# Third pair's routing re-spread over the last attention steps, with its stores on SyncE and its scaling on GpSimd

## The chip, the cores and the metric

The kernel runs on one core of one Trainium2 chip. A core has five engines that run at the same time, each working through its own queue of instructions in order: TensorE (matrix products), VectorE, ScalarE, GpSimd and SyncE, which here only issues transfers. Times are device microseconds (us) of the whole program, launch to end; lower is better.

## The reference

Sliding-window causal attention (window 64) is followed by a mixture of experts without dropped tokens: each token goes to the one expert with its largest logit, through that expert's two-layer network, and the result is scaled by the softmax weight of that expert.

```python
# q, k, v: batch 8, heads 8, sequence 576, head size 64
scores = scale * np.matmul(q, k.transpose(0, 1, 3, 2))
scores = np.where((rel >= 0) & (rel < 64), scores, -1e9)
attn = softmax(scores);  attn_out = np.matmul(attn, v)
x = attn_out.transpose(0, 2, 1, 3).reshape(4608, 512)
logits = x @ w_gate                        # 8 experts
expert_idx = np.argmax(logits, axis=1)
gate_w = probs[np.arange(N), expert_idx]
for e in range(8):                         # rows sorted by expert
    h = np.maximum(x_sorted[lo:hi] @ w1[e], 0.0)     # 512 -> 1024
    y_sorted[lo:hi] = h @ w2[e]                      # 1024 -> 512
return gate_w[:, None] * y_sorted[inv_perm]
```

## The kernel before

**Attention.** The batch is worked on in four pairs (bg 0 to 3), the heads in four groups of two (g). A pair and a group are a unit, 16 in all, and a unit has three steps of three tiles of 128 queries (a pair has nine tiles): N = 48 steps, s = 0 to 47. The function step (line 1013) writes out by hand, under a manual schedule, what every engine gets in step s, as a software pipeline. In order:

- scored(s+1), the score products into PSUM banks 0 and 1 (TensorE, L700); masked(s+1), mask and row maximum (VectorE, L713); softened(s+1), the exponential (ScalarE, L723);
- weighted(s-1), the product with v (TensorE, L746); logit(s-3), the gate's logits (TensorE, L783);
- flipped(s): TensorE transposes the probabilities of both heads (L731), and the results are copied out of PSUM, head 0 by VectorE, head 1 by ScalarE (pT, L733);
- divided(s-1), division by the sum (VectorE, L756 to L760), into xs;
- loads of later units, all issued by SyncE (L615, L627, L631, L638), with copies of v by GpSimd (L639 to L645);
- turned(s+3), transposes of q and k (TensorE, L659 and L667, with copies on ScalarE, L662 and L672; the third step of a unit has only two transposes); x_turned(s-2), transposes of xs (TensorE L771, copy on ScalarE L774);
- what the list todo holds for this step.

Transposed blocks go to PSUM banks 2 to 5 in rotation (tr_ring): the fifth user waits until the first one's bank has been copied out.

**Routing.** When a pair's logits are complete, after() (L950) puts its routing into the todo lists of the following steps. choose(bg) is a generator of five parts: the maximum; the one-hot of the expert (oh_all) and the exponentials; rank products on TensorE (L833) and the gate weights (L843 to L845); ranks within experts (L850 to L860, the fourth part); and position (L862 to L870, the fifth part: rkhi, low). place(j) then builds two one-hot matrices of a tile (lo, L874), weigh scales a tile of xs by its gate weight (L883 on ScalarE, L885 on GpSimd) and store writes chunks of three tiles to x_dram (L894, L901). For the third pair (bg = 2) after() is called for step 39: parts at steps 39, 39, 40, 41 and 41, places at 42 to 44, scaling at 41 to 44 with two tiles (m = 2 and 6) on ScalarE, stores at 42 to 44 issued by GpSimd.

**The first table.** first_tiles (L974), at the end of step 45, finds the tokens of expert 0's first two tiles among the first three pairs: VectorE forms key and hi_e (L976, L979), TensorE multiplies lo with hi_e in 54 small products (L986), VectorE turns the slots into token numbers (perm_e, L989), and gather_first (L290) clears a buffer and fetches the tokens' rows from x_dram with an indirect DMA on GpSimd. The tokens numbered past the third pair are left out by a bounds check.

**After the loop.** turn() (L312) transposes the fetched rows (L316) and the first expert tile starts, interleaved with the rest of the attention and the last pair's routing. sums_w2(0) (L142, GpSimd) forms sums of expert 0's second weights, which SyncE loads in two halves at steps 42 and 45 (L1048, shown as L1036 in the trace since todo runs them). Then gather_first is called for the second tile. The experts' products are arranged as seven block products instead of eight (hidden and output, L354 and L398), and fill the time from about 210 us to the end.

Of the kernel before, what the change touches and what calls it, by code (L numbers as in the profile page):

```python
# [24 lines left out]
def _ins(ap: bass.AP, axis: int, n: int) -> bass.AP:  # L25

    dims = [list(d) for d in ap.ap]
    dims.insert(axis, [0, n])
    return bass.AP(tensor=ap.tensor, offset=ap.offset, ap=dims)


def _inner(ap: bass.AP, n: int) -> bass.AP:
    return _ins(ap, len(ap.ap), n)
# [3 lines left out]
def kernel(  # L37
# [10 lines left out]
    nc = tc.nc  # L48
    P = nc.NUM_PARTITIONS
    B, H, S, D = q.shape  # L50
# [9 lines left out]
    SM = NV * P  # L60
    BG = 2
    NTB = BG * S // P
# [40 lines left out]
    V, G = nc.vector, nc.gpsimd  # L103
# [51 lines left out]
    def sums_w2(e):  # L155
        form(right_sums(G, s2s[e % NW], *w2q(e)))
# [23 lines left out]
    with tc.tile_pool(name="tmp", bufs=1) as tmp:  # L180
# [8 lines left out]
        for i in range(BG):  # L189
# [12 lines left out]
            out=before[:], in_=ones[:], pattern=[[1, P]], compare_op=ALU.is_gt, fill=0.0, base=0,  # L202
# [42 lines left out]
    ST = 3  # L245
# [12 lines left out]
    xg_all = qk_m(0, C, DM)  # L258
    xg = [xg_all[:, c] for c in range(C)]
# [29 lines left out]

    def gather_first(tokens):  # L290

        for c in range(C):
            G.memset(xg[c], 0.0)

            G.indirect_dma_start(
                out=xg[c], out_offset=None, in_=x_dram[0 : NT - BG * S, :],
                in_offset=bass.IndirectOffsetOnAxis(ap=tokens[:, c : c + 1], axis=0),
                bounds_check=NT - BG * S - 1, oob_is_err=False,
            )
# [144 lines left out]
    NQ = P // QD  # L444

    def half_tile(e, blocks, after, next_x):

        w1, w2 = w1s[e % NW], w2s[e % NW]
# [119 lines left out]
    with tc.manual_schedule(), ExitStack() as held, ExitStack() as brief:  # L568
# [51 lines left out]
        def load_rests(bg):  # L620

            at = 6144 + bg % 2 * 2048
            vr = qk_m(at + 1024, BG, H, D)
            rests[bg] = [qk_m(at, H, D), qk_m(at + 512, H, D), vr]
            for t, src, queue in zip(rests[bg], (q, k), (nc.sync, nc.sync if bg else nc.scalar)):
                for i in range(BG):
                    queue.dma_start(  # L627
                        out=t[i * D : (i + 1) * D], in_=src[bg * BG + i, :, SM:S, :].rearrange("h p d -> p h d")
                    )
            for i in range(BG):  # L630
                nc.sync.dma_start(out=vr[D:P, i], in_=v[bg * BG + i, :, SM:S, :].rearrange("h p d -> p h d"))  # L631

        def load_v(u):
            bg, g = units[u]
# [39 lines left out]
        def blocks_of(t):  # L674

            return [(t // NV, t % NV * 2 + a) if t < BG * NV else (a, NB - 1) for a in range(2)]
# [42 lines left out]
        def softened(prs, mx):  # L719
            for h in range(2):  # L720
                for m in range(ST):
                    y = prs[h][:, m, :]
                    nc.scalar.activation(out=y, in_=y, func=AF.Exp, scale=-1.0, bias=mx[:, h, m : m + 1])  # L723
            return prs

        def flipped(prs):
            pTs = []
            for h in range(2):
                tr = banks[next(tr_ring)](0, ST, P)
                for m in range(ST):  # L730
                    nc.tensor.transpose(out=tr[:, m, :], in_=prs[h][:, m, :], identity=ident[:])  # L731
                pT = att.tile([P, ST, P], F32, name=f"pT{h}")
                (nc.scalar.copy if h else nc.vector.tensor_copy)(out=pT[:], in_=tr[:])  # L733
                pTs.append(pT)
            return pTs

        def weighted(s, pTs):
            u, c = divmod(s, NST)
            bg, g = units[u]
            va, vb = v_ring[u % NVR]  # L740
            px = banks[6 if s < N - 2 else s - N + 2](0, 2, ST, VW)
            for m in range(ST):
                for a, (bp, i) in enumerate(blocks_of(c * ST + m)):
                    vt = va[:, bp, i // 2] if i % 2 or i == 0 else vb[:, bp, i // 2 - 1]
                    for h in range(2):
                        nc.tensor.matmul(  # L746
                            px[a * D : (a + 1) * D, h, m, :], lhsT=pTs[h][:, m, a * D : (a + 1) * D],
                            rhs=vt[:, h, :], start=True, stop=True, skip_group_check=True,
                        )
            return px  # L750
# [25 lines left out]
        def logit(s):  # L776

            u, c = divmod(s, NST)
            bg, g = units[u]
            if g == 0 and c == 0:  # L780
                lgs[bg] = banks[7](0, NST, P)[0 : ST * GE]
            for m in range(ST):
                nc.tensor.matmul(  # L783
                    lgs[bg][m * GE : (m + 1) * GE, c, :], lhsT=wg[:, g, :], rhs=xTs[s][:, m * P : (m + 1) * P],
                    start=(g == 0 and c == 0), stop=(g == NG - 1), skip_group_check=True,
                )
            return g == NG - 1
# [113 lines left out]
                    engine.dma_start(out=x_dram[t0 + SM : t0 + S, :], in_=x[i * D : (i + 1) * D, ST - 1, :])  # L901

        gates = {}
        todo = {}


        def slot_table(hi):
# [42 lines left out]
        def after(s, routing, bg):  # L950

            do = lambda n, op: todo.setdefault(s + n, []).append(op)
            part = lambda: next(routing, None)
            if bg < last - 1:
                for n in range(5):
                    do(n, part)

                for m in range(NTB):
                    do(5 + m * 2 // 3, partial(place, bg * NTB + m))
                    do(5 + m * 2 // 3, partial(weigh, bg, m, G))  # L960
                    if m % ST == ST - 1:
                        do(5 + m * 2 // 3, partial(store, bg, m // ST, G))
                return

            for n in (0, 0, 1, 2, 2):
                do(n, part)
            for m in range(NTB):
                do(3 + m // 3, partial(place, bg * NTB + m))
                do((2, 2, 3, 3, 4, 4, 4, 5, 5)[m], partial(weigh, bg, m, nc.scalar if m in (2, 6) else G))
                if m % ST == ST - 1:  # L970
                    do(3 + m // ST, partial(store, bg, m // ST, G))
            do(6, first_tiles)

        def first_tiles():  # L974

            V.scalar_tensor_tensor(  # L976
                out=key[:], in0=rkhi[:, 0:NJE], scalar=1.0, in1=oh_all[:, 0, 0:NJE], op0=ALU.add, op1=ALU.mult
            )
            V.tensor_tensor(  # L979
                out=hi_e[:], in0=_inner(key[:], NE * C), in1=_ins(hi_id[:, C + 1 : C + 1 + NE * C], 1, NJE),  # L980
                op=ALU.is_equal,
            )
            slots = banks[next(tr_ring)](0, NE * C)
            for j in range(NJE):
                for i in range(2):
                    nc.tensor.matmul(  # L986
                        slots, lhsT=lo[:, i, j], rhs=hi_e[:, j], start=(i + j == 0), stop=(i + j == NJE)
                    )
            V.tensor_scalar(out=perm_e[:], in0=slots, scalar1=-1.0, scalar2=float(NT), op0=ALU.mult, op1=ALU.add)  # L989
            gather_first(perm_e[:, 0:C])  # L990

        N = NU * NST
        load_qk(0)
# [18 lines left out]
        prs, pTs = {}, {}  # L1012
        def step(s):
            if 0 <= s + 1 < N:
                prs[s + 1] = softened(*masked(s + 1, scored(s + 1)))
            if 0 <= s - 1 < N:
                px = weighted(s - 1, pTs.pop(s - 1))
            ripe = 0 <= s - 3 < N and logit(s - 3)
            if 0 <= s < N:
                pTs[s] = flipped(prs.pop(s))  # L1020
            if 0 <= s - 1 < N:
                divided(s - 1, px)
            if s >= 0 and s % NST == 0:
                u = s // NST
                if u + 3 < NU and (u + 3) % NG == 0:
                    load_rests((u + 3) // NG)
                if u + 2 < NU:
                    load_v(u + 2)
                if u + 3 < NU:
                    load_qk(u + 3)  # L1030
            if s + 3 < N:
                turned(s + 3)
            if 0 <= s - 2 < N:
                x_turned(s - 2)
            for op in todo.pop(s, ()):
                op()  # L1036
            if ripe:
                bg, c = (s - 3) // (NG * NST), (s - 3) % NST
                parts = by_tokens(bg, c)
                next(parts)  # L1040
                todo.setdefault(s + 1, []).append(partial(next, parts, None))
                if c == NST - 1:
                    after(s + 1, choose(bg), bg)
# [4 lines left out]
            todo.setdefault(s, []).append(partial(nc.sync.dma_start, out=w2s[0][:, fs], in_=w2v[0][:, fs]))  # L1048
        for s in range(-3, N):
            step(s)  # L1050
        assert not todo
        sums_w2(0)


# [45 lines left out]
        table = slot_table(hi)  # L1100
# [144 lines left out]
```

## Time and profile before

| | |
|---|---|
| runs of the kernel | 700.83, 703.4, 706.3 us; median 703.4 |
| the profiled execution | 701.35 us |
| its span, first to last instruction | 699.6 us |
| mean granted TensorE clock | 0.993 |
| TensorE busy with products | 674.8 us, 96% |
| VectorE, ScalarE, GpSimd busy | 504.4, 262.3, 356.3 us |
| TensorE busy, 123 to 165 us | 41.26 of 42 |
| TensorE busy, 172 to 190 us | 16.33 of 18 |
| TensorE busy, 190 to 205 us | 11.70 of 15, at clock 0.79 |
| TensorE busy, 236 to 700 us | 454.70 of 464 |

In the profile PE is TensorE's products, PEld its weight loads, DVE VectorE, ACT ScalarE, POOL GpSimd and SP SyncE. L986 is line 986 of the kernel. A name with q (SPq, POOLq) is the engine's instruction queue. In a timeline row stand the start, the duration, engine, line, operation, what is written and read, and in brackets the idle time before it and what ended that. In a row of waits stand the waiting engine and line, what it waited for, and the total, the number and the longest in us. In a row of windows stand the stretch, its length, the busy time of PE, PEld, DVE, ACT and POOL, the granted TensorE clock as a share of full speed, the busy share of the DMA engines, and GB/s.

### The profile page before, as it was taken

How to read it: one execution, taken by the hardware profiler on the slowest of the kernel's cores; microseconds unless marked ns; L12 is line 12 of the kernel's file. 1: busy time of each engine (PE TensorE's matmuls, PEld its weight loads, DVE VectorE, ACT ScalarE, POOL GpSimd, SP SyncE). 2: the span in 40 equal slices, each digit the busy share in tenths (PEclk: the TensorE clock that was granted, in tenths of full speed). 3: DMA queues.
4: the chain of work that ended last, by engine and by line, in shares of the span. 5: the costliest groups of instructions: out<-in, count | busy, mean ns of one | idle time of the engine just before them, and what ended most of it. 6: DMA issues, size and time to landing. Idle time of an engine off the chain costs nothing. (4 is left out here: it accounts for less than half of the span.)

```text
span 699.6 us, 18016 instructions
## 1 busy us (share of the span) xinstructions
PE 674.8 (96%) x6894; PEld 590.8 (84%) x6894; DVE 504.4 (72%) x1657; ACT 262.3 (37%) x665; POOL 356.3 (51%) x368
## 2 busy tenths in 40 slices
PE   5999999999989999999999999999999999999996
PEld 4888888878769898897999899899789799789995
DVE  3667898898966958774866776676767576776864
ACT  5888889878745211111211111121121121132211
POOL 5414659387475025946662167267255757254012
PEclk9999999999989999999999999999999999999999
DMA  9988789887342281451711163171226171111022
GB/s 201 220 207 190 180 194 237 209 203 197 126 163 81 92 297 61 142 210 37 259 60 63 31 226 106 33 269 63 64 88 240 50 254 64 64 38 58 6 62 61
DMA packets 137151, 94.52 MB, mean 135 GB/s; under 512 B 116591, under 2 KB 116607, under 8 KB 137024
## 3 DMA queue, kind: packets, MB, share of 16 engines
q1 hardware_dynamic: 114752, 36.19, 21.1%
q0 software_dynamic: 9120, 28.60, 12.7%
q10 hardware_dynamic: 13152, 28.05, 11.6%
q8 instruction: 78, 1.28, 0.7%
q14 instruction: 49, 0.40, 0.2%
HBM read 73.94 MB, written 20.45 MB: 135 GB/s over the span
## 5 line engine op out<-in xcount | busy, mean ns | idle before, releaser
L325 DVE STREAM_TRANSPOSE v_m<-qk_m 32x256 f32<-32x256 f32 x320 | 139.2, 435 | 6.9 <-DMA qk_m<-x_dram,at_g 0.9
L285 POOL DMA_INDIRECT qk_m<-x_dram,at_g x42 | 45.0, 1072 | 161.5 <-DVE v_m L325 152.6
L354 PE MATMUL bank<-qk_m,s 128*128 128x128 f32 x1024 | 122.4, 275 | 0.0
L354 PEld LDWEIGHTS bank<-qk_m,s 128*128 128x128 f32 x1024 | 118.3, 192 | 0.0
L723 ACT ACTIVATE pr<-pr,mx 128x128 f32<-128x128 f32 x288 | 89.6, 390 | 31.6 <-DVE mx L713 31.2
L354 PE MATMUL bank<-qk_m,w 128*128 128x128 f32 x768 | 94.1, 276 | 0.8 <-PEq L1150 0.5
L354 PEld LDWEIGHTS bank<-qk_m,w 128*128 128x128 f32 x768 | 90.3, 192 | 4.3 <-issue 4.0
L713 DVE CUSTOM_DVE_ANT_0 pr<-bank,mask 128x128 f32<-128x128 f32 x288 | 64.4, 286 | 22.5 <-PE bank L700 20.4
L305 POOL DMA_INDIRECT out_dram<-v_m,at_s x42 | 42.6, 1013 | 57.1 <-DVE v_m L394 51.4
L394 DVE TENSOR_TENSOR v_m<-bank,v_m 128x256 f32<-128x256 f32 (+1 forms) x95 | 43.8, 480 | 37.8 <-PE bank L398 27.3
L641 POOL COPY v_m<-v_m 64x520 f32<-64x520 f32 x32 | 19.8, 617 | 67.0 <-DMA v_m<-in_v_dram 59.6
L142 POOL TENSOR_TENSOR s<-w 128x1024 f32<-128x1024 f32 x22 | 52.2, 2373 | 0.0
L746 PEld LDWEIGHTS bank<-v_m,pT 128*64 128x64 f32 x1152 | 41.1, 139 | 11.6 <-issue 4.5
L746 PE MATMUL bank<-v_m,pT 128*64 128x65 f32 x1152 | 48.2, 229 | 2.3 <-DVE xs L760 1.2
L398 PE MATMUL bank<-qkT_m,v_m 128*128 128x256 f32 x216 | 48.3, 379 | 0.0
L361 ACT COPY qk_m<-bank 128x512 f32<-128x512 f32 x16 | 9.4, 586 | 99.4 <-PE bank L354 73.4
L700 PE MATMUL bank<-qkT_m 64*64 64x128 f32 x1152 | 44.8, 282 | 1.0 <-DVE mx L713 0.8
L337 ACT COPY qk_m<-v_m 128x512 f32<-128x512 f32 x40 | 22.7, 615 | 61.4 <-DVE v_m L325 61.4
L398 PEld LDWEIGHTS bank<-qkT_m,v_m 128*128 128x128 f32 x216 | 41.0, 190 | 5.5
L731 PE MATMUL bank<-ident,pr 128*128 128x128 f32 x288 | 42.5, 284 | 0.0
L667 PE MATMUL bank<-ident,qk_m 128*128 128x128 f32 x256 | 35.2, 282 | 7.0 <-DMA qk_m<-in_q_dram 6.4
L364 DVE TENSOR_TENSOR qk_m<-bank,qk_m 128x512 f32<-128x512 f32 x16 | 11.1, 692 | 40.7 <-PE bank L354 40.7
(196 smaller groups left out, 1264.4 us busy)
## 6 DMA issues: line engine op xcount, KB each, us to landing
w<-in_moe_w_dram ACTq DMA_DIRECT2D x9, 2048.0 KB, 8.3
qk_m<-in_q_dram SPq DMA_DIRECT2D x72, 128.0 KB, 3.7
qk_m<-in_k_dram SPq DMA_DIRECT2D x66, 128.0 KB, 3.4
v_m<-in_v_dram SPq DMA_DIRECT2D x64, 128.0 KB, 3.2
qk_m<-in_moe_w_dram ACTq DMA_DIRECT2D x3, 2048.0 KB, 11.5
w<-in_moe_w_dram SPq DMA_DIRECT2D x2, 2048.0 KB, 14.1
x_dram<-xs POOLq DMA_DIRECT2D x6, 512.0 KB, 4.5
x_dram<-xs POOLq DMA_DIRECT2D x3, 768.0 KB, 5.2
```

The lines of the kernel that those rows point to most:

```text
L142: op()
L285: G.indirect_dma_start(out=xg[c], out_offset=None, in_=x_dram[:, :], in_offset=bass.IndirectOffsetOnAxis(ap=at_g[:, c : c + 1], axis=0),)
L305: put = G.indirect_dma_start(out=out[:, :], out_offset=bass.IndirectOffsetOnAxis(ap=at_s[:, c : c + 1], axis=0), in_=ys[c], in_offset=None ...
L325: V.transpose(out=xn[b * QD : (b + 1) * QD, :, :, a * QD : (a + 1) * QD].rearrange("p c g i -> p (c g) i"), in_=rows[a * QD : (a + 1) * QD ...
L354: nc.tensor.matmul(acc[:, f, :], lhsT=a[:, g, f * P : (f + 1) * P], rhs=b[:, g, :], start=(first and f == 0 and g == 0), stop=(g == HG - 1 ...
L394: plus = lambda out, a, b: V.tensor_tensor(out=out, in0=a, in1=b, op=ALU.add)
L398: nc.tensor.matmul(acc, lhsT=a[:, f, :], rhs=b[:, f, :], start=(start and f == 0), stop=(stop and f == HF - 1), skip_group_check=True,)
L700: nc.tensor.matmul(out_, lhsT=qT[rows, t, a * WINDOW : (a + 1) * WINDOW], rhs=rhs, start=True, stop=True, skip_group_check=True,)
L713: V.tensor_tensor_reduce(out=prs[h][:, m, :], in0=scs[h][:, m, :], in1=mask[:, m0 + m, :], scale=-scale, scalar=-2 * MASKED, op0=ALU.add, ...
L723: nc.scalar.activation(out=y, in_=y, func=AF.Exp, scale=-1.0, bias=mx[:, h, m : m + 1])
L731: nc.tensor.transpose(out=tr[:, m, :], in_=prs[h][:, m, :], identity=ident[:])
L746: nc.tensor.matmul(px[a * D : (a + 1) * D, h, m, :], lhsT=pTs[h][:, m, a * D : (a + 1) * D], rhs=vt[:, h, :], start=True, stop=True, skip_ ...
```

## The change

For the third pair alone (bg = 2): the fifth part of choose moves from step 41 to 42, and the places from 42 to 44 to 43 to 45. All nine scalings go to GpSimd, and the stores are issued by SyncE, in the same steps as before. first_tiles becomes a generator: key and hi_e stay at the end of step 45, and the products, perm_e and the gather move to step 46, behind scored(47) and weighted(45) and ahead of logit and flipped. In steps 41 to 45 ScalarE copies both heads' transposed probabilities out of PSUM. gather_first clears the whole buffer with one memset ahead of both gathers. Apart from that, the rows of v past the whole tiles of the first pair (L631 for bg = 0) are loaded by GpSimd's queue instead of SyncE's.

```diff
     def gather_first(tokens):
 
+        G.memset(xg_all, 0.0)
         for c in range(C):
-            G.memset(xg[c], 0.0)
-
             G.indirect_dma_start(
...
             for i in range(BG):
-                nc.sync.dma_start(out=vr[D:P, i], in_=v[bg * BG + i, :, SM:S, :].rearrange("h p d -> p h d"))
+                (nc.sync if bg else G).dma_start(out=vr[D:P, i], in_=v[bg * BG + i, :, SM:S, :].rearrange("h p d -> p h d"))
...
-        def flipped(prs):
+        def flipped(s, prs):
...
-                (nc.scalar.copy if h else nc.vector.tensor_copy)(out=pT[:], in_=tr[:])
+                (nc.scalar.copy if h or N - 7 <= s <= N - 3 else nc.vector.tensor_copy)(out=pT[:], in_=tr[:])
...
-            for n in (0, 0, 1, 2, 2):
+            for n in (0, 0, 1, 2, 3):
                 do(n, part)
             for m in range(NTB):
-                do(3 + m // 3, partial(place, bg * NTB + m))
-                do((2, 2, 3, 3, 4, 4, 4, 5, 5)[m], partial(weigh, bg, m, nc.scalar if m in (2, 6) else G))
+                do(4 + m // 3, partial(place, bg * NTB + m))
+                do((2, 2, 3, 3, 4, 4, 4, 5, 5)[m], partial(weigh, bg, m, G))
                 if m % ST == ST - 1:
-                    do(3 + m // ST, partial(store, bg, m // ST, G))
-            do(6, first_tiles)
+                    do(3 + m // ST, partial(store, bg, m // ST, nc.sync))
+            table = first_tiles()
+            do(6, partial(next, table))
+            between.setdefault(s + 7, []).append(partial(next, table))
 
         def first_tiles():
...
                 op=ALU.is_equal,
             )
+            yield
             slots = banks[next(tr_ring)](0, NE * C)
...
             gather_first(perm_e[:, 0:C])
+            yield
...
                 px = weighted(s - 1, pTs.pop(s - 1))
+            for op in between.pop(s, ()):
+                op()
             ripe = 0 <= s - 3 < N and logit(s - 3)
             if 0 <= s < N:
-                pTs[s] = flipped(prs.pop(s))
+                pTs[s] = flipped(s, prs.pop(s))
```

More of the change, by code (lines that the diff above doesn't have):

```diff
@@ L903 @@
         gates = {}
-        todo = {}
+        todo, between = {}, {}
         def slot_table(hi):
@@ L1050 @@
             step(s)
-        assert not todo
+        assert not todo and not between
         sums_w2(0)
```

## The prediction

> **What bounds the kernel now.** I read the page's busy shares first, then TensorE's waits in windows of the span, then windows of 2 to 4 us around the longest waits, then the timeline of each engine there.
>
> ```profile
> PE 674.8 (96%) x6894; PEld 590.8 (84%) x6894; DVE 504.4 (72%) x1657; ACT 262.3 (37%) x665; POOL 356.3 (51%) x368
> ```
>
> TensorE sets the time: what shortens its idle or slow stretches shortens the span, and other engines count only where TensorE waits for them. From 20 to 170 us it hardly waits. The waits of 172 to 212 us, where the third pair's routing (bg=2) lies beside the last pair's attention, are these:
>
> ```profile
> POOL x_dram L894 <- issue: 8.1, 1, 8.1
> POOL qk_m L295 <- DVE mx L713: 3.3, 1, 3.3
> PE bank L986 <- DVE hi_e L979: 2.7, 1, 2.7
> PE bank L771 <- DVE pT L733: 1.4, 1, 1.4
> PE bank L746 <- DVE xs L760: 0.5, 1, 0.5
> ```
>
> Two of TensorE's three waits are of one kind: VectorE is late. The windows (PE, PEld, DVE, ACT, POOL busy; then PEclk, the granted clock) show a third cost that no wait lists:
>
> ```profile
> 196.00:200.00 4.00, 1.29 (x32) 1.12 (x31) 3.15 (x21) 2.60 (x8) 3.70 (x5) 0.85 0.30 92
> 200.00:202.00 2.00, 2.00 (x58) 1.96 (x55) 0.16 (x1) 0.00 (x0) 0.32 (x1) 0.50 0.96 322
> 202.00:204.00 2.00, 2.00 (x35) 1.57 (x30) 1.35 (x12) 1.18 (x4) 0.42 (x1) 0.50 0.01 4
> 204.00:206.00 2.00, 2.00 (x15) 1.56 (x12) 0.62 (x2) 0.74 (x4) 1.73 (x3) 0.60 0.31 55
> 206.00:208.00 2.00, 1.96 (x35) 1.45 (x34) 0.76 (x3) 0.81 (x2) 1.97 (x2) 1.00 0.51 164
> ```
>
> After the idle stretch ahead of L986 the clock is half until about 205.5, so a busy TensorE is a slow one there. In TensorE's timeline a step begins at its L700 row:
>
> ```profile
> 184.29 0.55 PE L771 MATMUL bank<-ident,xs 128*128 128x128 f32 x3 [1.43 <-DVE pT L733]
> 184.77 0.89 PE L700 MATMUL bank<-qkT_m 64*64 64x128 f32 x24
> 199.31 1.58 PE L986 MATMUL bank<-hi_e,lo 128*128 128x4 bf16 x54 [2.71 <-DVE hi_e L979]
> 200.82 1.56 PE L700 MATMUL bank<-qkT_m 64*64 64x128 f32 x24
> 210.01 1.09 PE L316 MATMUL bank<-ident,qk_m 128*128 128x128 f32 x8
> ```
>
> L700 takes 1.56 us at half clock, 0.89 at full. Lost time by step: step 42 (179.06 to 184.77) 5.71 against 4.07 of step 43, so 1.6; step 45 (192.26 to 196.60) 4.3 against 3.2, so 1.1; the wait for hi_e 2.7; step 46 (200.82 to 206.11) 5.3 against 3.2, so 2.1. Together 7.5 us are in reach; the 54 matmuls of L986 (1.51) stay.
>
> **What the Trainium skill says.** "TensorE: Matmul & The Clock Gate", Part 1: an idle window of about 3.4 us sends the clock to half, and a busy window of that size brings it back. The trace agrees in kind: idle from 196.6, half from about 198.8 (2.2 us later), full at 205.5. "GPSIMD Engine Reference", Specifications: GpSimd shares its SBUF interfaces with VectorE, against two-input or two-port instructions. The trace agrees: lo<-...tok_b (L874) takes 0.31 us while GpSimd rests and 0.74 at 189 to 191 beside its scaling. "DMA: Bandwidth & Descriptors", Issuing engines are not separate DMA queues: SyncE's and GpSimd's transfers use the same 16 engines, so moving a store saves issue time, not transfer time. Nothing before contradicts it.
>
> **The change, part by part.** VectorE's fixed work in a step: masking 1.27 (6 x 0.21 from start to start), pT 0.47, division 0.90 (178.83 to 179.73). Routing: fourth part of choose 1.40 (179.73 to 181.13), fifth 1.29 (to 182.42), three places 1.33 alone (185.04 to 186.37) or 2.4 beside GpSimd (189.01 to 191.40), key and hi_e 0.45.
>
> *Fifth part to step 42, places to 43 to 45, pT of head 0 to ScalarE in 41 to 45.* VectorE's sum by step, against TensorE's 3.42, 4.07, 4.07, 3.42, 3.20: before 5.33, 2.64, 3.97, 5.04, 5.23 (22.2 of 18.2); after 3.57, 3.46, 4.57, 3.50, 3.95 (19.1), if only the places of step 43 meet GpSimd. The surplus that delays hi_e falls from 4 us to about 1.
>
> *All nine scalings on GpSimd.* Before, GpSimd did two (176.34 to 179.45) and then stood 8.07 us, since its next instruction, the store of chunk 0, waited for ScalarE's scaling of m=2 (186.26). Now nine run in a row: 9 x 1.56 = 14 us, to 190.5 instead of 197.6. That puts them beside the fourth and fifth parts, where GpSimd rested before. Neither is shown beside these scalings; for pair two, beside GpSimd's copies, the fifth took 2.7 (138.61 to 141.3), and pair one's fourth 2.1 (87.10 to 89.2). Bounds: +0 and +2.1. No gain is possible, since 1.40 and 1.29 are the undisturbed sizes.
>
> *ScalarE.* Five copies of 0.36 come, two scalings of 0.62 go: +0.6 in all. A full step has exp 1.77, copies 0.72, 0.96 and 0.37: 3.82 of 4.07, so it does not bind by sum. But head 0's copy now stands behind the exp of the next step, and x_turned in a full step reuses its PSUM bank 4 rotations later: it is ready 3.47 after the step's start, TensorE needs it at 3.65. So any masking over 0.2 late stalls TensorE in steps 42 and 43.
>
> *Walking the four queues through steps 41 to 47* gives the first turn (L316, 210.01 before): undisturbed, step 43 begins at 183.3, 45 at 190.8, 46 at 194.2, L986 ends 198.0, turn at 203.1: gain 6.9. With the fourth and fifth parts slowed: stalls of about 0.8 and 0.7 in steps 42 and 43, step 45 at 192.25, 46 at 195.7, hi_e at 197.85 (L986 waits 0.2), L986 ends 199.45, turn at 204.6: gain 5.4. In both the longest idle stretch is under 1 us, below the 1.43 that left the clock full at 184. I take the middle, 6.1.
>
> *Table behind the next scores.* L986 moves past scored(47) and weighted(45), 1.7 us of work that covers hi_e; without it L986 would wait about 1.9. Behind it on TensorE stand logit, flipped and all else. What comes late next is the gather: before, perm_e was ready at 201.16 but the gather began at 203.58, when the last store (issued 199.21, landing about 4.4 later) was in. Now perm_e is ready 0.3 after L986, 199.75; gathers start at about 200.05 and 201.1 (1.03 each) and land 3.5 after issue: 203.6 and 204.6. TensorE wants them at 204.6 and 205.1. Hidden with 0.5 to spare; up to 1 lost.
>
> *Stores on SyncE.* GpSimd loses six issues (4.05 us); SyncE issues them at 0.37 to 0.5. Behind them in SyncE's queue stands only w2's second half: its issue goes from 188.9 to about 192.3, landing near 198. sums_w2 on GpSimd follows the gathers at about 202: covered by 4 us. The last store, issued about 192, lands near 197, before perm_e.
>
> *One memset for two* (1.08 instead of 2 x 0.54): the first is off the path, done at about 191.6, and the second gather has 4 us of slack (issued 218.60, used 226.14). Nothing.
>
> *v's rest rows of the first pair on GpSimd.* SyncE's queue shortens by 1.31 us, so q, k and v of the first units are issued earlier. TensorE waited 0.80 at 18.30 for GpSimd's copies of v. But the DMA engines are 0.87 to 0.89 busy in 0 to 20 us, and the rows now leave behind wg and the zero row (9.35 us) instead of at 6.55. Bounds: 0.8 gained, 0.5 lost if they land after v; I take 0.2 gained.
>
> Sum: 6.1 + 0.2 = 6.3 us. From 210 us on TensorE is busy to 98%, and the rest moves up whole. The profiled execution took 701.35 (span 699.6 and 1.75 around it), so 695.0 on that footing. It lies 2.05 under the median of the three runs (703.4); the middle of the four is 702.4, and I forecast from there: **696**.
>
> **Rivals.** (1) *VectorE stays late.* GpSimd now scales through 14 us without a pause; if it slows the places of steps 44 and 45 too (2 x 1.0) besides the 2.1 above, hi_e comes 2 us late, TensorE idles over 2.2 and the clock halves again: the hi_e wait falls little and the 2.1 stays lost. Of 7.5, 2.5 to 3 are won: 699.5. For: the 0.74 rows. Against: by 190.5 the scalings are done. (2) *The gather comes last, slower than before.* SyncE's last store shares the engines with w2's megabyte; SyncE's largest loads took 14.1 us to land (w, 2 MB). A store that took 14 would be in at 206, the second gather at 210.6: 5.5 idle at the turn, and after 2.2 idle the clock is half for some 6 us, 2.5 more: 8 lost against 6.3 won, 704. It decides from a gather 3.8 us late. Against: stores landed in at most 6.5 beside w2's load. (3) *Nothing disturbs*: 6.9 + 0.8, 694.7, and to 693 if the runs lie low like the profiled one.
>
> **How the numbers follow.** Forecast 0.55, rival 1 0.2, rival 2 0.08, rival 3 0.17. The runs of before spread 5.5 us, so about 1% (7 us, 696.4) is what a measurement can tell from no change; the forecast lies on that edge. Faster by over 1%: half of the forecast and most of rival 3, about 0.5; slower by over 1% (710) needs a gather 10 us late or a misread mechanism, 0.06. The range reaches from rival 3 with low runs, 691.5, to rival 1 with high ones, 701.
>
> **What would show it.** Right: L986 waits under 0.5; PEclk 1.00 from 196 to 206; no 8 us pause on GpSimd, scalings in a row to about 190.5; L316 first at 203 to 205; small waits of L771 for ScalarE's pT in steps 42 and 43. Wrong: a wait at L316 or L986 over 2 us, a clock of 0.50 near either, fourth and fifth parts over 2.7 each, or a first v copy later than 17.06.

## The result, and the profile after

The changed kernel takes 694.5 us (median of 4 runs, 693.43 to 694.98) against 702.31 for the kernel before (4 runs beside it, 700.83 to 706.3): a ratio of 0.9878, 95% interval 0.9833 to 0.9923. The medians differ by 7.8 us here, and by about 7 beside the larger sets of the kernel before, whose medians are 701.6 to 702.0. The forecast was 696. The profiled execution took 694.91, span 693.1, mean granted clock 0.999 instead of 0.993.

The page's busy row shows TensorE's share up from 96% to 97% for the same products:

```profile
PE 672.6 (97%) x6894; PEld 589.1 (85%) x6894; DVE 501.7 (72%) x1652; ACT 263.1 (38%) x668; POOL 357.4 (52%) x364
```

The waits of 165 to 212 us: the 2.7 us for hi_e and the 1.4 for VectorE's pT are gone. The longest wait of TensorE's products is 0.7, now for ScalarE's pT, and what was GpSimd's 8.1 us pause at a store is an 8.5 us wait for perm_e, with its other work done.

```profile
POOL qk_m L294 <- DVE perm_e L991: 8.5, 1, 8.5
...
PE bank L770 <- ACT pT L732: 0.8, 2, 0.7
...
PEld bank L315 <- DMA qk_m<-x_dram,perm_e: 0.3, 1, 0.3
```

The windows of the same stretch (columns as before: the busy times, then the granted clock). Where it was 0.50, it is 1.00:

```profile
196.00:200.00 4.00, 3.91 (x92) 3.41 (x92) 2.78 (x17) 2.72 (x8) 1.16 (x1) 1.00 0.17 62
200.00:202.00 2.00, 2.00 (x25) 1.40 (x21) 0.85 (x4) 0.54 (x2) 1.86 (x2) 1.00 0.54 152
202.00:204.00 2.00, 1.96 (x31) 1.60 (x30) 1.45 (x4) 0.79 (x2) 1.92 (x2) 1.00 0.39 111
```

TensorE's timeline after, from the third pair's rank products to the turn (most lines are one lower than before; L986 is now L988):

```profile
174.45 0.20 PE L832 MATMUL bank<-oh_all,before 128*128 128x72 bf16 x1 [0.25 <-ACT pT L732]
...
186.97 0.55 PE L770 MATMUL bank<-ident,xs 128*128 128x128 f32 x3 [0.65 <-ACT pT L732]
...
194.07 0.89 PE L699 MATMUL bank<-qkT_m 64*64 64x128 f32 x24
...
196.03 1.50 PE L988 MATMUL bank<-hi_e,lo 128*128 128x4 bf16 x54
...
202.84 1.36 PE L315 MATMUL bank<-ident,qk_m 128*128 128x128 f32 x8
```

The turn begins at 202.84, 7.17 us earlier than 210.01. Before, the rank products of step 40 stood at 175.47: 1.02 us was gained ahead of them, and the stretch from them to the turn fell from 34.54 to 28.39, 6.15 us. This stretch is the measure used below, since it leaves out what happens at the start. (Steps are numbered as in the prediction: in the profile after, step 42 begins at 178.04.) The expert tiles move up nearly whole: 6.9 us at 228, 6.5 at the end.

GpSimd's timeline after: nine scalings in a row, and two gathers that wait for the table and for no store.

```profile
175.32 13.91 POOL L884 TENSOR_SCALAR xs<-xs,gate 128x512 f32<-128x512 f32 x9 [1.32 <-DVE gate L844]
189.18 0.94 POOL L292 MEMSET qk_m<- 128x1024 f32 x1
198.65 1.16 POOL L294 DMA_INDIRECT qk_m<-x_dram,perm_e  x1 [8.53 <-DVE perm_e L991]
200.12 1.02 POOL L294 DMA_INDIRECT qk_m<-x_dram,perm_e  x1 [0.30 <-issue]
```

SyncE issues the last store at 190.45 and w2's second half at 191.98; the third pair's six stores land 2.7 to 4.1 us after their issue, the last one after 3.8, ahead of perm_e (197.63).

### The profile page after: what moved, and what is told of

Read it like the earlier page. It is cut to its first block, busy times and chain, and to the rows that moved or that the text cites. A ratio compares the mean times of both kernels' runs of the same rounds, so it can differ in the third digit from the quotient of the medians.

```text
span 693.1 us, 18015 instructions
## 1 busy us (share of the span) xinstructions
PE 672.6 (97%) x6894; PEld 589.1 (85%) x6894; DVE 501.7 (72%) x1652; ACT 263.1 (38%) x668; POOL 357.4 (52%) x364
## 5 line engine op out<-in xcount | busy, mean ns | idle before, releaser
L884 POOL TENSOR_SCALAR xs<-xs,gate 128x512 f32<-128x512 f32 x27 | 41.9, 1564 | 2.0 <-DVE gate L844 1.3
```

## The experiments

Twelve kernels: four add one part to the kernel before, four take one part out of the changed kernel, two change an idle stretch, one is the changed kernel again, one is a variation. The single memset is in every kernel whose name begins with a, in none that begins with b, and is not tested alone. They ran on three chips, each kernel beside its own runs of before (medians 701.58, 702.03 and 701.74). "Stretch" is rank products to first turn (its first half, where it comes in two) in the one execution that was profiled; "idle" is TensorE's longest wait there, with its line's work.

| kernel | median us (runs) | ratio to before, 95% | stretch | idle |
|---|---|---|---|---|
| before | 701.6 to 702.3 | 1 | 34.54 | 2.71 at the table |
| b_start | 699.52 (20) | 0.9965 to 0.9987 | 33.83 | 2.71 at the table |
| b_table | 704.07 (20) | 1.0007 to 1.0049 | 33.22 | 1.89 + 1.00 at the turn |
| b_spread | 700.44 (12) | 0.9956 to 1.001 | 31.65 | 2.71 at the table |
| b_store | 706.77 (7) | 1.0047 to 1.0108 | 36.78 | 2.55 in step 42, 1.90 at the table |
| b_fill | 708.59 (6) | 1.0013 to 1.0094 | 33.21 | 0.71 + 1.72 at the turn |
| changed | 694.5 (4) | 0.9833 to 0.9923 | 28.39 | 0.65 in step 43 |
| a_same | 694.8 (6) | 0.9851 to 0.9914 | 28.37 | 0.64 in step 43 |
| a_rest | 693.71 (6) | 0.9833 to 0.9893 | 28.49 | 0.32 in step 46 |
| a_notable | 697.37 (12) | 0.9925 to 0.9956 | 32.38 | 1.89 at the table |
| a_nospread | 698.19 (12) | 0.9938 to 0.9965 | 32.08 | 2.54 in step 42 |
| a_nostore | 700.04 (20) | 0.9959 to 0.9986 | 31.12 | 2.64 + 0.67 at the turn |
| a_vec | 697.92 (9) | 0.992 to 0.9967 | 32.60 | 0.71 at the table |
| a_late6 | 698.42 (10) | 0.9925 to 0.9976 | 33.66 | 2.96 at the table |

**The start alone (b_start)**: the kernel before, with the first pair's rest rows of v on GpSimd.

```diff
-                nc.sync.dma_start(out=vr[D:P, i], in_=v[...])
+                (nc.sync if bg else G).dma_start(out=vr[D:P, i], in_=v[...])
```

> The kernel before, with v's rest rows of the first pair loaded from GpSimd's queue and nothing else. Theory (the loads at the start gave the 1.0 us by which step 40 begins earlier, 169.95 for 170.97): step 40 at 170.0 within 0.2, the first turn at 209.0, the time 1.0 lower. Rival (the start gave only the 0.4 us seen at 24 us, and the wait of 0.63 for k at 51 us is scatter of the run): step 40 at 170.5 or later, the time 0.4 lower, not to be told from none.

It gains 2.1 us in the medians, twice what was expected, and leaves the table's wait of 2.71 as it was. Up to the table's products the stretch is the same as before, 23.84 us. Behind them it is 0.71 shorter, since the same wait halves the clock for 3.41 us here and for 6.83 (198.76 to 205.59) in the profile of before. Windows of b_start:

```profile
198.87:202.28 3.41, 3.41 (x56) 2.58 (x46) 1.39 (x13) 1.86 (x6) 1.02 (x1) 0.50 0.25 73
202.28:205.69 3.41, 3.41 (x47) 2.80 (x46) 1.71 (x5) 0.86 (x2) 3.11 (x4) 1.00 0.46 135
```

So 0.7 us of a stretch can be a matter of where the profiled execution's clock changes fell; the last section comes back to this. The reason for the gain at the start is seen in other kernels that keep the old start. Waits of TensorE from 0 to 30 us in b_store:

```profile
PE bank L667 <- DMA qk_m<-in_q_dram: 5.5, 1, 5.5
PE bank L746 <- DMA v_m<-in_v_dram: 2.8, 2, 1.7
```

And in the changed kernel:

```profile
PE bank L666 <- DMA qk_m<-in_q_dram: 6.3, 2, 6.2
PE bank L745 <- POOL v_m L644: 0.6, 1, 0.6
```

With the old start TensorE can wait for the first loads of v themselves (up to 3.1 us in sum, in b_fill; with the new start at most 0.9, in a_vec). In four of the five profiles with the old start the clock is then half for 3.41 or 6.83 us, somewhere between 18.2 and 25.7 us; in none of the nine with the new start is it. The score products that follow these waits begin at 20.65 in the profile of before, but at 22.22 in b_table, 23.40 in b_store, 23.78 in b_fill and 24.04 in b_spread; with the new start they begin at 19.59 to 20.23 in all nine profiles. The rank products follow: 175.47, 177.37, 177.45, 178.09 and 177.78 (b_fill) with the old start, 172.49 to 175.25 with the new one. The profile of before happened to be the earliest of the old starts. The new start also narrows the times: 3.1 us from lowest to highest in 20 runs of b_start, against 6.4 in 50 of before and 8.4 in 20 of b_table.

**The table alone (b_table)**: the kernel before, with the table's products behind the next scores.

```diff
-            do(6, first_tiles)
+            table = first_tiles()
+            do(6, partial(next, table))
+            between.setdefault(s + 7, []).append(partial(next, table))
```

> The kernel before, with the first table's products, token numbers and gather moved behind the next scores, and nothing else. Theory (parts need each other: GpSimd's stores land late, so the gather becomes the last): the wait of TensorE for hi_e falls from 2.7 to about 1.0 and the clock stays at 1.00, worth 3.8, but the gathers still begin at 203.6 when the stores are in, and the first turn waits 2 to 3 us for them: turn's second half at about 209, 1 to 1.5 us won. Rival (VectorE's lateness is all): the turn at 206.2, 3.8 won, no wait at the turn.

It is slower by 0.07 to 0.49%, where 1 to 1.5 us were expected to be won. The cover works: the products begin with no wait for hi_e and the clock is full behind them. But the gather cannot use the earlier table. GpSimd's timeline:

```profile
201.10 0.56 POOL L901 DMA_DIRECT2D x_dram<-xs  x1
...
206.96 1.13 POOL L295 DMA_INDIRECT qk_m<-x_dram,perm_e  x1 [4.76 <-issue]
```

The last store is issued at 201.10 and lands 4.7 us later, and the gather starts 1.2 after that. TensorE's timeline shows the price at the turn:

```profile
210.59 0.66 PE L316 MATMUL bank<-ident,qk_m 128*128 128x128 f32 x4 [1.89 <-DMA qk_m<-x_dram,perm_e]
212.25 0.66 PE L316 MATMUL bank<-ident,qk_m 128*128 128x128 f32 x4 [1.00 <-DMA qk_m<-x_dram,perm_e]
```

From the rank products to the end of the turn it takes 35.5 us, as before (35.6), and the half clock is back as well, from 212.8 to 216.2, in front of the experts instead of behind the table.

**The spread alone (b_spread)**: the fifth part and the places a step later, and ScalarE's copies.

```diff
-                (nc.scalar.copy if h else nc.vector.tensor_copy)(out=pT[:], in_=tr[:])
+                (nc.scalar.copy if h or N - 7 <= s <= N - 3 else nc.vector.tensor_copy)(out=pT[:], in_=tr[:])
...
-            for n in (0, 0, 1, 2, 2):
+            for n in (0, 0, 1, 2, 3):
...
-                do(3 + m // 3, partial(place, bg * NTB + m))
+                do(4 + m // 3, partial(place, bg * NTB + m))
```

> The kernel before, with the fifth part of choose and the places a step later and head 0's copy on ScalarE in steps 41 to 45, and nothing else. Theory: the stall of 1.4 in step 42 goes, VectorE does 2.3 us less before hi_e, but TensorE comes earlier too, so the wait for hi_e stays near 2.3 and the clock still halves: turn 2.3 earlier, near 207.7. Rival (the spread alone is the gain): wait for hi_e under 0.7, clock 1.00, turn at 205 or earlier.

The stretch is 2.9 us shorter. Of these, 2.2 lie ahead of the table's products, where the stall of step 42 is now 0.15; the rest is a half clock that lasts 3.41 us instead of 6.83, as in b_start. The table's wait is still 2.71, and the clock still halves behind it. The median is 1.1 lower, and the interval includes no change.

**GpSimd and SyncE alone (b_store)**: nine scalings on GpSimd, stores issued by SyncE.

```diff
-                do((2, 2, 3, 3, 4, 4, 4, 5, 5)[m], partial(weigh, bg, m, nc.scalar if m in (2, 6) else G))
+                do((2, 2, 3, 3, 4, 4, 4, 5, 5)[m], partial(weigh, bg, m, G))
...
-                    do(3 + m // ST, partial(store, bg, m // ST, G))
+                    do(3 + m // ST, partial(store, bg, m // ST, nc.sync))
```

> The kernel before, with all nine scalings on GpSimd and the stores issued by SyncE, and nothing else. Theory: GpSimd scales without a pause from 176 to 190.5, the fourth and fifth parts of choose grow from 2.7 to about 4 together beside it (stall in step 42 from 1.4 to about 2.5), the places of steps 43 and 44 shrink by about 1.5 in sum, and the turn moves by less than 1 us either way. Rival (GpSimd's late stores set the end already): turn 2 us or more earlier.

A larger loss than expected, 5.2 us in the medians. TensorE's waits (175 to 218 us) and three of its windows:

```profile
PE bank L771 <- DVE pT L733: 2.5, 1, 2.5
PE bank L986 <- DVE hi_e L979: 1.9, 1, 1.9
```

```profile
186.91:193.73 6.82, 6.33 (x66) 5.17 (x67) 5.06 (x25) 4.97 (x15) 5.79 (x5) 0.50 0.26 90
193.73:203.97 10.24, 8.34 (x164) 6.96 (x163) 8.89 (x47) 7.15 (x21) 0.00 (x0) 1.00 0.54 174
203.97:210.80 6.83, 6.83 (x102) 5.65 (x100) 2.89 (x17) 2.50 (x8) 4.49 (x4) 0.50 0.27 80
```

Scalings without a pause lie beside both routing parts that VectorE does in step 41, and pT comes 2.5 late instead of 1.4. That brings a half clock of its own (186.9 to 193.7), and the table's wait a second one (204.0 to 210.8). The stretch grows by 2.2. Not all of the 5.2 us is the part's: the profiled run is the slowest of the seven (710.46), and its last scatter is issued by 699.4, 9.3 us before the end of the span, against 4.1 to 4.8 us in every other profile. The runs stand in two groups, four at 705.3 to 706.8 and three at 709.9 to 710.5; the lower four alone give a loss of 4.5 us. What the 5 us at the end are stays open.

The four parts alone come to −2.1 + 2.5 − 1.1 + 5.2 = +4.5 us (+3.8 with the lower group of b_store); together they give −7 to −7.8.

**The changed kernel without one part.** a_notable puts the table back to the end of step 45, a_nospread the spread, a_nostore the stores on GpSimd and m = 2 and 6 on ScalarE, each the reverse of the diff above. a_vec puts back only head 0's copies to VectorE:

```diff
-                (nc.scalar.copy if h or N - 7 <= s <= N - 3 else nc.vector.tensor_copy)(out=pT[:], in_=tr[:])
+                (nc.scalar.copy if h else nc.vector.tensor_copy)(out=pT[:], in_=tr[:])
```

> The changed kernel, with the whole first table back at the end of step 45. Theory: TensorE reaches the table's products 1.7 earlier than now and waits 1.9 for hi_e, long enough to halve the clock in step 46, as 1.90 was in the run with GpSimd's part alone: 1.9 and about 2 lost, 3.5 to 4 us over the changed kernel. Rival (1.9 idle does not halve the clock after all): 1.5 to 2 over.

> The changed kernel, with the fifth part back in step 41, the places in 42 to 44 and head 0's copy back on VectorE. Theory: the fourth and fifth parts together grow beside GpSimd's scaling, step 42 stalls 2.5 and the clock halves there, as in the run with GpSimd's part alone: 5 us or more over the changed kernel, PEclk 0.50 between 184 and 190. Rival (with the table moved there is room for it): under 3 over, clock 1.00.

> The changed kernel, with m=2 and 6 scaled by ScalarE and the stores issued by GpSimd again. Theory: GpSimd pauses some 5 us for ScalarE's m=2, its last store is issued near 198 and lands near 203, so the gathers begin 3 to 4 us later than 198.65 and the first turn waits 3 to 4 for them, the clock halving behind: 5 to 6 us over the changed kernel. Rival (the stores were not what the gather waited for): within 1.5 of the changed kernel.

> The changed kernel, with head 0's transposed probabilities copied by VectorE in all steps. Theory: VectorE gets 5 x 0.47 = 2.35 more before hi_e, so the table's products wait about 2 us, with or without the clock halving: 2 to 4 us over the changed kernel; the small waits of L770 for ScalarE turn into waits for VectorE of about the same size. Rival (VectorE had slack by then, ScalarE's copies only cost): same time or less than the changed kernel.

Against 694.5: a_notable costs 2.9 us, a_nospread 3.7, a_nostore 5.5, a_vec 3.4. The stretch grows by 3.99, 3.69, 2.73 and 4.21 (in a_nostore to the first half of the turn; its second half waits again). a_nostore came as expected; a_notable's stretch too, with a little less in the time. a_nospread cost less than the 5 us or more expected. a_vec's time lies where it was expected, but not for the reason given: the table's wait is 0.71 instead of about 2, and the rest is small waits for VectorE (0.66 and 0.71 for pT, twice 0.48 for xs) and a half clock.

In a_notable the wait is 1.89, as the prediction had it for a table without its cover, and the clock is 0.50 from 195.0 to 201.8. In a_nostore the old pause is back (6.07), the last store leaves at 196.88, and the turn waits:

```profile
206.37 0.63 PE L315 MATMUL bank<-ident,qk_m 128*128 128x128 f32 x4 [2.64 <-DMA qk_m<-x_dram,perm_e]
207.67 1.11 PE L315 MATMUL bank<-ident,qk_m 128*128 128x128 f32 x4 [0.67 <-DMA qk_m<-x_dram,perm_e]
```

In a_nospread the stall is that of b_store, 2.54 for VectorE's pT, but the half clock expected from it isn't there. It comes at 199.37, about the table, where TensorE idled only 0.48. Windows of a_nospread, the first two meeting inside the wait (180.79 to 183.33):

```profile
178.89:182.30 3.41, 1.90 (x20) 1.51 (x14) 3.17 (x17) 0.16 (x1) 3.41 (x4) 1.00 0.74 279
182.30:185.72 3.42, 2.26 (x51) 1.78 (x51) 3.35 (x17) 3.40 (x10) 3.42 (x3) 1.00 0.46 172
...
195.96:199.37 3.41, 2.93 (x88) 2.61 (x86) 2.33 (x16) 2.60 (x9) 0.00 (x0) 1.00 0.03 10
199.37:202.78 3.41, 3.41 (x33) 2.96 (x33) 1.38 (x4) 0.96 (x2) 2.39 (x3) 0.50 0.23 61
```

a_vec does the same after small waits: 0.48 and 0.71 on both sides of 24 products, then the 54 small ones, then half clock from 200.15 to 203.56.

```profile
196.68 1.02 PE L745 MATMUL bank<-v_m,pT 128*64 128x65 f32 x24 [0.48 <-DVE xs L759]
198.41 1.49 PE L988 MATMUL bank<-hi_e,lo 128*128 128x4 bf16 x54 [0.71 <-DVE hi_e L980]
...
200.19 1.54 PE L730 MATMUL bank<-ident,pr 128*128 128x128 f32 x6
```

**Is it the idle time that halves the clock?** b_fill adds 22 needless transposes to the kernel before, where TensorE idles ahead of the table; a_late6 adds six needless VectorE additions ahead of key and hi_e in the changed kernel (and clears their tile once at the start), to make it idle there.

```diff
+            bank = banks[next(tr_ring)]
+            for n in range(22):
+                nc.tensor.transpose(out=bank(P, P), in_=ident[:], identity=ident[:])
-            slots = banks[next(tr_ring)](0, NE * C)
+            slots = bank(0, NE * C)
```

```diff
+            for n in range(6):
+                V.tensor_tensor(out=of[:], in0=of[:], in1=of[:], op=ALU.add)
             V.scalar_tensor_tensor(
                 out=key[:]
```

> The kernel before, with 22 needless transposes of the identity into an unused part of the table's bank ahead of the table's products, some 2.7 to 3 us of work where TensorE idles for hi_e. Theory (the half clock of step 46 comes from that idle time): hi_e no later, L986 begins at most 0.4 later, the clock stays 1.00, step 46 takes 3.2 instead of 5.3, the first turn comes some 1.5 to 2 earlier against L833. Rival (the light products of L986 or something else halve it): clock 0.50 behind L986 as before, turn 0 to 0.4 later.

> The changed kernel, with six needless VectorE additions (288 elements, about 0.4 us each, 2.4 us) ahead of key and hi_e. Theory: L988 waits 2.2 to 2.6 and the clock halves behind it as in the kernel before: turn 4 to 4.5 later than in the changed kernel, time 3 to 4.5 higher. Rival (the clock follows a free-running window, so that an idle time of 2.5 may pass unpunished, as in the run without the spread): turn only 2.2 to 2.6 later in the trace, and times in two groups.

b_fill says yes for the clock: with the idle stretch filled, 2.71 becomes 0.31, and the clock stays at 1.00 from 196 to 208. Windows of b_fill:

```profile
204.00:208.00 4.00, 3.98 (x70) 3.08 (x71) 2.73 (x16) 2.60 (x8) 0.60 (x1) 1.00 0.06 15
208.00:212.00 4.00, 2.93 (x37) 2.22 (x37) 2.29 (x7) 1.18 (x3) 3.70 (x4) 1.00 0.43 125
212.00:216.00 4.00, 2.64 (x15) 1.93 (x16) 0.89 (x3) 0.93 (x3) 3.92 (x3) 0.68 0.03 10
```

The stretch falls by only 1.3, since the gather (begun at 207.40, stores first) becomes the next wait, 0.71 and 1.72, and takes the half clock with it (213.5 to 216.9). Its times stand in two groups, two runs at 703.1 to 703.2 and four at 708.1 to 710.3, and its profile has 3.3 us of pauses at L501 late in the run, where the other profiles have at most 1.0; why stays open, so its time says nothing on the clock. a_late6 brings a wait of 2.96 and half clock from 197.9 to 204.7. The stretch grows by 5.3 over a_same, which is the wait and 2.3 more, put down here to the slow clock; the median grows by 3.6, and its ten runs show no two groups. So stretches of one execution and medians of ten agree in sign and order here, not to the us.

**Can the last stall go too?** a_rest lets GpSimd pause after the fourth scaling until VectorE has done the fifth part, by one tiny copy that needs low; a_same is the changed kernel beside it.

```diff
                 do((2, 2, 3, 3, 4, 4, 4, 5, 5)[m], partial(weigh, bg, m, G))
+                if m == 3:
+                    do(3, lambda: G.tensor_copy(out=pause[:], in_=low[:, bg * NTB : bg * NTB + 1]))
```

> The changed kernel, with GpSimd copying one column of low between the scalings of m=3 and m=4, so that it rests while VectorE does the fifth part. Theory (the fifth part takes 2.57 us instead of 1.29 because GpSimd works beside it, and the stores have a spare us): GpSimd pauses 1.2 to 1.5, the fifth part falls to about 1.4, the wait of 0.65 in step 43 goes, the turn comes 0.7 to 1.0 earlier against L832, and the gather still begins right after perm_e. Rival (the stores have nothing to spare): the gather begins later and the turn waits about 1 us: no gain or a loss.

> The changed kernel as it is, to be compared with the next on the same chip and with the parts. All theories: ratio to before near 0.989, first turn 28.4 us after the rank products of step 40 (L832), the clock not below 1.00 between them.

The pause is 1.44 and the wait of 0.65 in step 43 is gone, but the scalings now end at 191.2, beside the places of step 44, and the stretch is 28.49 against 28.37. The median is 1.1 us lower with overlapping intervals, and the profile shows no gain that would explain it. It is not shown to be better.

## Why the prediction was right

**What was lost where.** Right: the 7.5 us in reach were three waits and a half clock. (All three waits of TensorE that the prediction lists, not two, are for VectorE.) Of the stretch to the turn, 6.15 was won; the walk gave 5.4 with the routing slowed and 6.9 without. That the middle, 6.1, was met so closely is luck in part: the profile of before has two clock windows at half behind the table, and b_start, the same up to there, has one. Against b_start's stretch the changed kernel wins 5.44, and 5.0 in the medians. After, steps 42 and 43 last 4.47 and 4.94 instead of 4.07, so 0.40 and 0.87 lost where 0.8 and 0.7 were forecast; step 45 takes 3.20.

**VectorE beside GpSimd.** Inside the bounds. The fourth part takes 1.65 (177.72 to 179.37; bounds 1.40 and 2.1), the fifth 2.57 (181.53 to 184.10; up to 2.7), step 43's places 2.22 (2.4 forecast), those of steps 44 and 45 1.33 and 1.34, undisturbed as forecast. GpSimd's scalings end at 189.2 (190.5 forecast).

**The table and the gather.** Right in kind: products without a listed wait, perm_e at once followed by the gather. The margin was smaller than said: not 0.5 to spare but 0.3 late, at the second half of the turn, within the "up to 1 lost". a_nostore shows what the margin rests on: with the stores on GpSimd and two scalings on ScalarE the last store leaves at 196.88 instead of 190.45, the turn waits 3.31 us in two pieces, and the time is 5.5 higher. Two readings were off without harm: the 4.4 us from the last store to the gather of before were 3.2 to its landing and 1.2 more, and the third pair's stores landed in at most 4.8 us there, while the 6.5 belongs to an earlier pair.

**The start.** The mis-sized term. It was put at 0.2 with bounds of 0.5 lost and 0.8 gained; b_start measures 2.1. The mechanism was named (SyncE's queue shortens, v is issued earlier), but its worth was read from one profile, in which v happened to be in time and TensorE waited only 0.80 for a copy. Other profiles with the same start wait 1.9 to 3.1 for the loads themselves (b_spread, b_store, b_fill). With 2.1 in its place the sum is 8.2 and the forecast 694.2, against 694.5 measured. That is nearer than the parts are: in the medians b_start is worth 2.1 and all the rest 5.0, and the larger sets of before lie somewhat under the 702.4 that the sum starts from. An early start in the profile of before would also explain why the profiled spans differ by 6.5 and the medians by 7.8.

**The clock.** The sum used that idle stretches under 1.43 leave the clock full. In the changed kernel it held (0.65 at most), but as a safety it fails: a_vec halved after 0.48 and 0.71. Nor were the 2.2 us from the start of the idle stretch to the half clock, which rival 1 used, a delay: they are where that execution's clock windows fell (last section). The cover at the table is thinner than the prediction took it to be; without the copies on ScalarE it is gone, and 3.4 us with it.

**The rivals.** Both mechanisms are real, and in each kernel that lacks a part one of them appears: VectorE late in b_start, b_spread, b_store, a_notable, a_nospread and a_vec; the gather last in b_table and a_nostore (and in b_fill). The change escapes both because its parts cover each other: the earlier table pays only if the stores are out, stores and scalings off ScalarE pay only if VectorE's parts are spread, and the spread leaves hi_e late unless the table waits behind the next scores. The losses from taking out one part add to 12.1 for table, spread and stores, more than the whole gain; in each of the three profiles a half clock comes with the loss.

## What to carry to other kernels

When several waits stand close behind each other on one path, cost the edits as one walk through all queues: here three of four parts alone were slower or not measurably different, and together they gave 7 to 7.8 us. Size a part at the start of a program from several executions, since one profile shows one arrival of the first loads and not their scatter. Count a TensorE wait before light products as dear: the wait itself and often 1.4 to 2.3 us more of half clock behind it, of which one profile shows only one case, since the next execution's clock windows fall elsewhere.

## What was not expected of the hardware

- **The clock follows fixed windows, not the length of one wait.** In each of the 14 profiles the granted clock changes only at moments that lie a whole number of 3.413 us apart: in b_store, shown above, at 186.91, 193.73, 203.97 and 210.80, which are 2, 3 and 2 such windows. The twelve half clocks between 170 and 217 us last one window (six) or two (six). So the price of a wait depends on where it falls: the 2.54 of a_nospread was cut by an edge at 182.30, left 1.90 and 2.26 us of products in the two windows, and cost no clock, while the 2.71 of before left 1.25 in one window. One window at half cost about 1.4 us (the 2.1 of step 46 less b_start's 0.71), two cost 2.1 (before) to 2.3 (a_late6).
- **How full a window must be.** Counting the 54 small products (4 columns each) as nothing, the window ahead of each of the twelve half clocks was busy with products for at most 0.46 of its time, and every other window from 174 to 217 us at full clock for at least 0.49. Counted in full, the windows ahead of it in a_nospread and a_vec were busy for 0.86 and 0.79, while windows of 0.55 and 0.58 stayed full, so here the small products seem to count for little. b_table, with the same order of 0.48 idle, 24 products and 54 small ones as a_nospread, had the small ones cut by an edge at 202.53 and kept full clock. This is a fit to these profiles and not a test, and the limit isn't sharp: later windows of 0.45 (b_fill, 507) and 0.43 (a_nospread, 687) stayed full. By it the changed kernel is clear wherever the windows fall (at least 0.52 in any 3.41 us from 174 to 202, an estimate from its profile) and a_rest isn't (0.44). The Trainium skill, "TensorE: Matmul & The Clock Gate", Part 1, says that the window is about 3.4 us long and free-running, so that it does not reset when a kernel starts; the profiles agree. Where it says that an idle window brings the half clock, the measurement differs: windows filled to 0.35 (b_table), 0.40 (b_store) and 0.45 (a_notable), without any of the small products, did so.
- **GpSimd's scaling slows VectorE very unevenly.** Single instructions of the routing take 0.59 to 0.74 us beside it (L858, L861, L867, L869) where they took 0.17 to 0.23 in the profile of before, and lo up to 0.74 instead of 0.31, while L853 and L859 stay at 0.23 and masking at 0.21 from start to start. In a_rest, with GpSimd paused, the fifth part takes about 1.4 instead of 2.57. The Trainium skill, "GPSIMD Engine Reference", Specifications, names two-input and two-port VectorE instructions as those that contend, which the two-input L858 and L861 agree with; L859 has two inputs too and was not slowed, and L867, L869 and lo have one: whether they use two ports no trace here shows.
- **Moving two loads of 128 KB at the start is worth 2 us in the median** and halves the scatter of the whole kernel's times (from 6.4 us in 50 runs and 8.4 in b_table's 20, to 3.1 in 20).
